# Sixty-four rows of w_down in one load of eight partitions, at the end of a one-token transformer block

## The chip, the cores and the metric

The kernel runs on one core of a Trainium2 chip. The metric is the device time of one execution in microseconds; before the change its median is 407.73 us over 3 runs (407.71 to 407.74). Engines: PE (matrix products, with PEld for its weight loads), DVE (vector), ACT (activation), POOL (general), SP (issues the loads). Loads run on 16 transfer engines that all queues share.

## The reference

One token goes through attention over a cached context of 65,536 positions and then through a gated feed-forward part. All tensors are bf16.

```python
def _A_ref(x, k_cache, v_cache, wq, wo):        # x 1x1x1024, 32 query heads, 4 key heads, Dh = 128
    q = (x @ wq).reshape(B, Sq, Hq, Dh).transpose(0, 2, 1, 3)
    k = jnp.repeat(k_cache, rep, axis=1)
    v = jnp.repeat(v_cache, rep, axis=1)
    scores = jnp.einsum("bhqd,bhkd->bhqk", q, k) * (Dh ** -0.5)
    p = _softmax(scores, axis=-1)
    o = jnp.einsum("bhqk,bhkd->bhqd", p, v)
    return o.transpose(0, 2, 1, 3).reshape(B, Sq, Hq * Dh) @ wo

def _B_ref(x, w_gate, w_up, w_down):            # 1024 -> 3584 -> 1024
    return (_gelu(x @ w_gate) * (x @ w_up)) @ w_down

h = x + _A_ref(_layernorm(x), A_k_cache, A_v_cache, A_wq, A_wo)
h2 = h + _B_ref(_layernorm(h), B_w_gate, B_w_up, B_w_down)
```

## The kernel before, in words

All weights and both caches are read once, 173 MB. SP issues every load (`load`, L172) into `ring`, a buffer of three slots of 64 KB per partition. The order of the loads is fixed by the program: wq, the K and V pieces of 8 MB, wo (8 MB), w_gate and w_up (7 MB each), and then w_down in five pieces. A load waits until the products that read its slot's earlier content are done; the loads behind it on SP wait with it. All w_down pieces lie in the slot that wo had.

PE and DVE work through what has landed: K pieces are transposed by DVE (L288) and multiplied (`k_scores`), V pieces are multiplied with the softmax weights (`v_values`). Each engine works through its instructions in program order, apart from where the tile scheduler puts small independent ones.

The part that matters here is w_down, the last matrix. Its 3584 rows are split so that partition p has rows 28p to 28p + 27; the 28 rows of a partition are called c = 0 to 27. The activations `act_bf` (128 x 28, L544) are copied into `actz` (L547 with `padded`, L235), where each column is followed by 31 zero columns, so that a product gives 32 output rows of which the first counts. A product for one c contracts over the 128 partitions. Four row groups of PE (32 columns of weights each) work side by side: `row_mm` (L468) puts c into group c mod 4.

The order at the end is this:
- `keep_busy(4)`, L578. `keep_busy` (L557) makes products into `w_ps` that nobody reads.
- c = 0 to 15 come in one load (4096 KB, L580). Each c takes two products of 512 columns, which are added into the two banks `at_ps` (L582). These banks already hold the residual and the attention output. The last four c close the sums.
- `keep_busy(3)`, L583.
- `rows_out` (L486) copies the two banks to `sum_r`: DVE copies one, ACT the other (L248).
- Sixteen products with `ones_f` add the four row groups of `sum_r` up and start the sums in `f_ps` and `fb_ps`, one bank for each half of the output (L587).
- `keep_busy(4)`, L588.
- c = 16 to 23 (2048 KB), then `keep_busy(3)`, then c = 24 to 26 (768 KB): `down_rows` (L570) makes eight products of 128 columns for each c, into `f_ps` and `fb_ps`.
- c = 27 comes in two loads, one for each half of the columns (128 KB each, L597). After the first half four products into `f_ps` and a cast by DVE; after the second four into `fb_ps` and a cast by ACT (L601). Then SP stores the row (L602).

All five w_down loads are issued together once wo's slot is free.

Of the kernel before, what the change touches and what calls it, by code (L numbers as in the profile page):

```python
# [9 lines left out]
ALU = mybir.AluOpType  # L10
AX = mybir.AxisListType
BF16 = mybir.dt.bfloat16
F32 = mybir.dt.float32
PSUM = bass.MemoryType.PSUM
# [3 lines left out]
def kernel(  # L18
# [13 lines left out]
    nc = tc.nc  # L32
    P = 128
    D = A_x.shape[-1]
# [4 lines left out]
    F = B_w_gate.shape[1]  # L39
    DC = D // P  # L40
    FC = F // P
# [5 lines left out]
    CW = 16384  # L47
    NSLOT = 3
# [25 lines left out]
    sel = lead.tile([P, 32], F32, name="sel")  # L74
# [9 lines left out]
    o_fin = lead.tile([P, D // 4], BF16, name="o_fin")  # L84
    assert 2048 + 2 * 512 + 2 * 256 + 128 + 2 * 64 + 4 * 32 == ring_at - const_at - 128
    chpool = ctx.enter_context(tc.tile_pool(name="chpool", bufs=1))
    ring = chpool.tile([P, NSLOT * 2 * CW], BF16, name="ring")
    top = ctx.enter_context(tc.tile_pool(name="top", bufs=1))
    wsel = top.tile([P, W0 + NS * P], BF16, name="wsel", tag="wo")
    small = ctx.enter_context(tc.tile_pool(name="small", bufs=2))  # L90
# [1 line left out]
    def pt_tile(i, shape, dtype, name):  # L92
        return (lead if i == 0 else top).tile(shape, dtype, name=name, tag=f"pT{i}")
# [50 lines left out]
    def pe(op):  # L144
        return keep(op, "pe")
# [7 lines left out]
    def mm(out, lhsT, rhs, start, stop, loaded=False, tile_position=None, skip_group_check=False):  # L153
        t = nc.tensor
        if not loaded:
            return pe(t.matmul(out, lhsT=lhsT, rhs=rhs, start=start, stop=stop, tile_position=tile_position,  # L156
                               skip_group_check=skip_group_check))
        op = t.add_instruction(mybir.InstMatmult(  # L158
            name=nc.get_next_instruction_name(), engine=t.engine, start_tensor_calc=start, stop_tensor_calc=stop,
            tile_size=(lhsT.shape[0], lhsT.shape[1]), tile_position=tile_position or (0, 0), ldweights=False,  # L160
            bass_skip_group_check=skip_group_check,
            ins=[t.lower_ap(rhs), t.lower_ap(lhsT, for_matmul_weights=True)], outs=[t.lower_ap(out, opt=True)]))
        reuses.add(op.ins.name)
        return pe(op)
# [4 lines left out]
    slot = [NSLOT - 1]  # L169
    loads, pools, last = [], [], {}  # L170

    def load(src, off=0):  # L172
        n, w = src.shape[1], src.shape[2]
        if off == 0:
            slot[0] = (slot[0] + 1) % NSLOT
        assert off + n * w <= 2 * CW
        o = slot[0] * 2 * CW + off
        tv = ring[:, o:o + n * w].rearrange("p (n w) -> p n w", w=w)
        loads.append(nc.sync.dma_start(out=tv, in_=src).ins)
        return tv  # L180

# [2 lines left out]
    nc.scalar.dma_start(out=x_row[0:97:32, :], in_=A_x[0, 0].rearrange("(g n) -> g n", g=4))  # L184
    assert DC * HD == 2 * CW
    wq_t = load(wq_v[:])

    make_identity(nc, ident_bf[:])
# [12 lines left out]
    for bp in range(4):  # L201
        s0 = 64 * (bp // 2) + bp % 2
        nc.vector.tensor_copy(out=esel[:, bp, :, :],
                              in_=ident_bf[:, s0:s0 + 63:2].unsqueeze(1).to_broadcast([P, 4, 32]))

    one = ctx.enter_context(tc.tile_pool(name="one", bufs=1))
# [28 lines left out]
    def padded(i, vec, ncols, name):  # L235
        t = pt_tile(i, [P, ncols, 32], BF16, name)
        pools.append(nc.gpsimd.memset(t[:], 0.0))
        nc.vector.tensor_copy(out=t[:, :, 0], in_=vec)
        return t
# [7 lines left out]
    def evac(dst, src, k):  # L247
        return nc.vector.tensor_copy(out=dst, in_=src) if k % 2 == 0 else nc.scalar.copy(out=dst, in_=src)  # L248
# [27 lines left out]
    def kv_load(what, g, li, n):  # L276
        t = load((k_v if what == "k" else v_v)[g][:, li * LN:(li + n) * LN, :])
        for u in range(n):
            state[(what, g, li + u)] = t[:, u * LN:(u + 1) * LN, :]
# [130 lines left out]
    for n, u in enumerate(units):  # L410
# [24 lines left out]
        if g == 0 and li == NL - 1:  # L435
            softmax_turn(0)
            softmax_bias(0)
            for i, m in zip((NL - 1, 0, 1, 2), (2, 3, 4, 4)):
# [11 lines left out]
                            pattern=[[-1, OQ], [1, P]], channel_multiplier=-OQ)  # L450
# [8 lines left out]
    actx.close()  # L459
    ps_a = ctx.enter_context(tc.tile_pool(name="ps_a", bufs=2, space=PSUM))  # L460
    ps_w = ctx.enter_context(tc.tile_pool(name="ps_w", bufs=2, space=PSUM))
    ps_f = ctx.enter_context(tc.tile_pool(name="ps_f", bufs=1, space=PSUM))
    DS = D // 512

    def row_bank(name):
        return ps_w.tile([P, 512], F32, name=name, tag="w")

    def row_mm(banks, stat, w2, c, first, last):  # L468
        g = c % 4
        for s in range(DS):  # L470
            mm(banks[s][32 * g:32 * g + 32, :], stat, w2[:, s * 512:(s + 1) * 512], first, last,
               loaded=(s > 0), tile_position=(0, 32 * g), skip_group_check=True)
# [3 lines left out]
    assert Hq * D == 2 * CW  # L476
    at_ps = [ps_a.tile([P, 512], F32, name="at_ps", tag="a") for _ in range(DS)]
    wv = load(wo_v[:])
    for c in range(Hq):
        row_mm(at_ps, o2z[:, c, :], wv[:, c, :], c, c < 4, False)  # L480
# [5 lines left out]
    def rows_out(name):  # L486
        t = low.tile([P, DS, 512], F32, name=name, tag="sc0")
        for s in range(DS):
            last["act"] = evac(t[:, s, :], at_ps[s][:], s)
        return t  # L490
# [18 lines left out]
    def turned(banks, name, tag):  # L509
# [2 lines left out]
            nc.vector.transpose(out=t[:, k, :], in_=banks[k][:, 0:HF * 32])  # L512
        return t[:].rearrange("p k (j i) -> p (k j) i", i=32)[:, :, 0]

    g_banks = [row_bank("wg_ps") for _ in range(2)]
    gv = B_w_gate.rearrange("(p c) n -> p c n", c=DC)
    uv = B_w_up.rearrange("(p c) n -> p c n", c=DC)
# [25 lines left out]
    act_bf = top.tile([P, FC], BF16, name="act_bf")  # L543
    nc.vector.tensor_tensor(out=act_bf[:], in0=turned(u_banks, "wu_t", "sc2"), in1=gl[:], op=ALU.mult)  # L544

    wd_v = B_w_down.rearrange("(p c) n -> p c n", p=P)
    actz = padded(3, act_bf[:], FC, "actz")  # L547
    w_ps = row_bank("w_ps")

    def seen_by_sync(ins):  # L550
        seen = nc.sync.nop()
        for i in ins:
            tc.add_manual_dep(seen.ins, i.name,
                              mybir.DependencyInfo(mybir.DependencyClass.Sync, mybir.DependencyReason.DATA),
                              reason="seen")

    def keep_busy(n, src):  # L557
        for i in range(n):
            mm(w_ps[:], ident_bf[:], src, True, True, loaded=(i > 0))

    HW = D // 2
# [8 lines left out]
    def down_rows(wv, c0, n, bs):  # L570
        for cc in range(n):
            c = c0 + cc
            for g in range(4):
                for b in bs:
                    o = (b if len(bs) > 1 else 0) * HW + g * QW
                    half_mm(b, g, actz[:, c, :], wv[:, cc, o:o + QW], False, c + 1 == FC, loaded=(b > bs[0]))

    keep_busy(4, wu[:, 0, 0:512])  # L578
    c0 = 16
    wv = load(wd_v[:, 0:c0, :])  # L580
    for c in range(c0):
        row_mm(at_ps, actz[:, c, :], wv[:, c, :], c, False, c + 4 >= c0)  # L582
    keep_busy(3, wv[:, 0, 0:512])  # L583
    sum_r = rows_out("sum_r")
    for g in range(4):
        for b in range(2):
# [2 lines left out]
    for sz, nb in ((8, 3), (3, 0)):  # L589
        wv = load(wd_v[:, c0:c0 + sz, :], c0 * D)  # L590
# [3 lines left out]
    assert c0 == FC - 1  # L594
    o_b = o_fin[:].rearrange("p (b j) -> p b j", b=2)
    for b, put in ((0, nc.vector.tensor_copy), (1, nc.scalar.copy)):
        wv = load(wd_v[:, c0:FC, b * HW:(b + 1) * HW], c0 * D + b * HW)  # L597
        down_rows(wv, c0, 1, [b])
        if b == 1:
            seen_by_sync(loads[-8:] + [last["act"].ins] + [x.ins for x in pools])  # L600
        put(out=o_b[0:97, b, :], in_=halves[b][0:97, :])  # L601
    nc.sync.dma_start(out=out[0, 0].rearrange("(b g n) -> g b n", b=2, g=4),  # L602
                      in_=o_b[0:97:32, :, :])
# [30 lines left out]
```

## Time and profile before

| | |
|---|---|
| median of 3 runs | 407.73 us (407.71 to 407.74) |
| profiled execution, its own time | 407.8 us |
| its span, first to last instruction | 406.0 us |
| mean granted PE clock | 0.891 |
| read from memory | 173.02 MB, 426 GB/s over the span |
| PE, DVE, ACT, POOL busy | 73%, 50%, 10%, 2% of the span |
| 4096 KB of w_down first used | 395.56 us |
| last load landed, as the chain of waits has it | 402.84 us |
| store issued | 403.46 us |

Times within the profile count from the start of the span, 0 to 406.0 us. The row of busy tenths cuts the span into 40 slices of about 10 us, and a 9 means 90% or more. "PEclk" is the clock that the throttle granted, in tenths of full speed (in the windows as a fraction). "DMA" is the mean busy share of the 16 transfer engines. In a timeline row, the bracket at the end says how long the engine was idle before and what ended that. "L156" is the helper that makes products, "L158" the same for products that reuse the weights already loaded; so rows are told apart by their tiles: `at_ps`, `w_ps`, `f_ps`, `fb_ps`.

### The profile page before, as it was taken

The numbers are of one execution on the slowest core, as the hardware profiler recorded it, in microseconds if no ns is written. First come the engines' busy times: TensorE is split into PE (matmuls) and PEld (weight loads), VectorE is DVE, ScalarE is ACT, GpSimd is POOL, SyncE is SP. The second block draws the span as 40 slices with busy tenths as digits, with TensorE's granted clock in tenths as the row PEclk, the third lists the DMA queues.
The fourth block names the chain that finished last, engine by engine and source line by source line (L and its number), as shares of the span: only waits on it lengthen the run. The fifth ranks groups of instructions, "written<-read, shape, count | busy, mean of one in ns | idle before, by whom it ended". The sixth has DMA issues, their size and how long they took to land.

```text
span 406.0 us, 2610 instructions
## 1 busy us (share of the span) xinstructions
PE 295.5 (73%) x1519; PEld 59.4 (15%) x681; DVE 203.8 (50%) x186; ACT 40.0 (10%) x62; POOL 7.5 (2%) x17
## 2 busy tenths in 40 slices
PE   0160777758899695979969957997696999646196
PEld 0110111111111110221111113111110211211012
DVE  0210989999839744971595387609943000220210
ACT  1000000023000031100000302000021100100000
POOL 2000000000000000000000000000010000000000
PEclk9995689987899999769999967899999699886689
DMA  9999999999999999999999999999999999999995
GB/s 413 413 413 471 458 413 415 413 466 452 413 421 420 471 439 413 428 420 471 433 420 428 420 465 433 420 435 420 458 433 420 441 420 458 399 442 447 400 423 225
DMA packets 3631, 173.18 MB, mean 427 GB/s; under 512 B 416, under 2 KB 676, under 8 KB 804
## 3 DMA queue, kind: packets, MB, share of 16 engines
q1 hardware_dynamic: 3612, 173.02, 98.7%
q8 instruction: 8, 0.13, 0.1%
q14 instruction: 3, 0.02, 0.0%
q10 hardware_dynamic: 8, 0.00, 0.0%
HBM read 173.02 MB, written 0.00 MB: 426 GB/s over the span
## 4 chain that ended last, share of the span: by engine, by line
DMA 41%; PE 35%; DVE 21%; ACT 2%; issue 1%; ACTq 0%; DVEq 0%
DMA ring<-in_A_k_cache_dram 30%; DVE ring L288 16%; PE acc_ps L158 16%; DMA ring<-in_B_w_down_dram 11%; PE qk_ps L156 6%; PE qk_ps L158 5%; PE acc_ps L156 5%; DVE mx L313 2%; ACT sc L309 2%; DVE pT L346 1%; PE o_ps L156 1%; PE at_ps L156 1%; DVE acc_sb L369 1%; PE at_ps L158 1%; PE nb_ps L156 0%
## 5 line engine op out<-in xcount | busy, mean ns | idle before, releaser
L288 DVE STREAM_TRANSPOSE ring<-ring 128x2048 uint32<-128x2048 uint32 x64 | 142.6, 2279 | 36.9 <-DMA ring<-in_A_k_cache_dram 36.9
L156 PE MATMUL qk_ps<-ring,wsel 128*128 128x512 bf16 x256 | 107.4, 420 | 50.2 <-DVE ring L288 31.2
L158 PE MATMUL qk_ps<-ring,wsel 128*128 128x512 bf16 x256 | 106.6, 416 | 0.0
L158 PE MATMUL acc_ps<-ring,pT 128*128 128x512 bf16 x384 | 105.1, 383 | 0.0
L156 PEld LDWEIGHTS <-wsel 128*128 128x128 bf16 x256 | 27.1, 106 | 157.3 <-issue 140.4
L156 PE MATMUL acc_ps<-ring,pT 128*128 128x512 bf16 x128 | 49.1, 384 | 0.0
L313 DVE TENSOR_REDUCE mx<-qk_ps 128x1 f32<-128x1024 f32 x16 | 19.5, 1220 | 24.7 <-ACT sc L309 18.7
L346 DVE STREAM_TRANSPOSE pT<-pT 128x1024 bf16<-128x1024 bf16 x16 | 19.3, 1228 | 23.8 <-ACT pT L340 23.8
L309 ACT COPY sc<-qk_ps 128x1024 f32<-128x1024 f32 x12 | 12.1, 1012 | 149.5 <-PE qk_ps L158 149.5
L156 PEld LDWEIGHTS <-pT 128*128 128x128 bf16 x128 | 12.8, 100 | 90.7 <-issue 90.6
L369 DVE COPY acc_sb<-acc_ps 32x512 f32<-32x512 f32 x8 | 5.3, 667 | 29.4 <-PE acc_ps L158 29.3
L340 ACT ACTIVATE pT<-sc,nbias 128x1024 bf16<-128x1024 f32 x12 | 13.7, 1141 | 44.9 <-DVE nbias L332 41.9
L156 PE MATMUL wu_ps<-ring,hnz 128*32 128x448 bf16 x32 | 5.9, 729 | 9.0 <-DMA ring<-in_B_w_up_dram 9.0
L156 PE MATMUL ln_tot<-ln_s,ones_f 128*128 128x1 f32 x8 | 1.9, 312 | 13.5 <-DVE ln_s L210 11.7
L156 PE MATMUL q_ps<-ring,xnz 128*32 128x512 bf16 x32 | 5.0, 598 | 8.9 <-DMA ring<-in_A_wq_dram 8.9
L156 PE MATMUL wg_ps<-ring,hnz 128*32 128x448 bf16 x32 | 5.9, 718 | 7.2 <-DMA ring<-in_B_w_gate_dram 7.2
L156 PE MATMUL o_ps<-sel,acc_sb 128*128 128x8 f32 x32 | 6.6, 335 | 5.8 <-DVE rl L383 5.4
L371 ACT COPY acc_sb<-acc_ps 32x512 f32<-32x512 f32 x8 | 4.6, 578 | 58.6 <-DVE acc_sb L369 58.5
L512 DVE STREAM_TRANSPOSE wu_t<-wu_ps 128x448 f32<-128x448 f32 x2 | 1.2, 630 | 14.2 <-PE wu_ps L156 14.2
L261 DVE STREAM_TRANSPOSE q_t<-q_ps 128x512 f32<-128x512 f32 x2 | 1.3, 694 | 13.8 <-PE q_ps L158 13.8
L512 DVE STREAM_TRANSPOSE wg_t<-wg_ps 128x448 f32<-128x448 f32 x2 | 1.2, 628 | 13.4 <-PE wg_ps L156 13.4
L340 ACT ACTIVATE pT<-qk_ps,nbias 128x1024 bf16<-128x1024 f32 x4 | 4.5, 1114 | 29.8 <-PE acc_ps L158 16.8
(108 smaller groups left out, 94.2 us busy)
## 6 DMA issues: line engine op xcount, KB each, us to landing
ring<-in_B_w_gate_dram SPq DMA_DIRECT2D x1, 7168.0 KB, 35.5
ring<-in_B_w_up_dram SPq DMA_DIRECT2D x1, 7168.0 KB, 38.6
ring<-in_B_w_down_dram SPq DMA_DIRECT2D x1, 4096.0 KB, 39.6
ring<-in_B_w_down_dram SPq DMA_DIRECT2D x1, 2048.0 KB, 43.6
ring<-in_B_w_down_dram SPq DMA_DIRECT2D x1, 768.0 KB, 45.0
ring<-in_B_w_down_dram SPq DMA_DIRECT2D x2, 128.0 KB, 44.8
ring<-in_A_k_cache_dram SPq DMA_DIRECT2D x8, 38.6
ring<-in_A_v_cache_dram SPq DMA_DIRECT2D x8, 34.4
```

The lines of the kernel that those rows point to most:

```text
L156: return pe(t.matmul(out, lhsT=lhsT, rhs=rhs, start=start, stop=stop, tile_position=tile_position, skip_group_check=skip_group_check))
L158: op = t.add_instruction(mybir.InstMatmult(name=nc.get_next_instruction_name(), engine=t.engine, start_tensor_calc=start, stop_tensor_calc ...
L261: nc.vector.transpose(out=q_t[:, k, :], in_=q_banks[k])
L288: dv(nc.vector.transpose(out=kt[:, c * w:(c + 1) * w], in_=kt[:, c * w:(c + 1) * w]))
L309: ac(nc.scalar.copy(out=sc[:], in_=flat))
L313: dv(nc.vector.tensor_reduce(out=state[("mx", g)][:, li:li + 1], in_=flat, axis=AX.X, op=ALU.max))
L340: ac(nc.scalar.activation(out=flat, in_=state.pop(("sc", g, li)), func=ACT.Exp, bias=st["nbias"][:, 0:1], scale=scale, accum_out=st["lpart ...
L346: dv(nc.vector.transpose(out=flat, in_=flat))
L369: dv(nc.vector.tensor_copy(out=acc_sb[sl, :], in_=acc[sl, c, :]))
L371: ac(nc.scalar.copy(out=acc_sb[sl, :], in_=acc[sl, c, :]))
L512: nc.vector.transpose(out=t[:, k, :], in_=banks[k][:, 0:HF * 32])
```

## The change

Of c = 27, one row in each of 128 partitions, the rows of the odd partitions (64 rows of 1024 columns, 128 KB) come in a load of their own, issued behind the 4096 KB load. It goes to eight partitions (0, 8, ..., 56), eight rows to each, into the slot that w_gate had. The rows of the even partitions still come last, in two loads of half the columns, now of 64 partitions and 64 KB each.

The activations for the moved rows have to be moved to those eight partitions. A mask `part` spreads column 27 of `act_bf` over eight columns (`act_q`), one product with a 0/1 matrix `spread` gathers them in `act_ps`, and DVE copies them, padded with zeros, to `few`. Eight rows then make sixteen products of 512 columns into `at_ps`, behind `keep_busy(3)` and ahead of the copies to `sum_r`; they now close the sums there. Column 27 of `actz` is set to zero for odd partitions through the mask `even`. `spread`, `part` and `even` are made once, early. The three slots of `ring` become three tiles. The number of products after each of the two last loads stays four.

```diff
-    ring = chpool.tile([P, NSLOT * 2 * CW], BF16, name="ring")
+    ring = [chpool.tile([P, 2 * CW], BF16, name=f"ring{i}") for i in range(NSLOT)]
...
+    ps_s = ctx.enter_context(tc.tile_pool(name="ps_s", bufs=1, space=PSUM))
...
+    KQ = 8
+    KR = P // 2 // KQ
+    KW = P // KQ
+    low_rows = B_w_down.rearrange("(q r c) n -> q r c n", q=KQ, c=2 * FC)[:, :, 2 * FC - 1, :]
+    part = one.tile([P, KR], F32, name="part", tag="gmb")
+    even = top.tile([P, 1], F32, name="even")
+    spread = top.tile([P, P], BF16, name="spread", tag="wo")
+    nc.vector.tensor_reduce(out=part[:], in_=sel[:].rearrange("p (x r t) -> p t r x", r=KR, t=2)[:, 1], axis=AX.X, op=ALU.add)
+    nc.vector.tensor_reduce(out=even[:], in_=sel[:, 0::2], axis=AX.X, op=ALU.add)
+    nc.gpsimd.memset(spread[:], 0.0)
+    ones_at = spread[:, 0:8 * KQ:8]
+    nc.gpsimd.memset(ones_at, 1.0)
+    nc.gpsimd.affine_select(out=ones_at, ...)
+    nc.gpsimd.affine_select(out=ones_at, ...)
...
-    actz = padded(3, act_bf[:], FC, "actz")
+    FL = FC - 1
+    actz = pt_tile(3, [P, FC, 32], BF16, "actz")
+    pools.append(nc.gpsimd.memset(actz[:], 0.0))
+    nc.vector.tensor_copy(out=actz[:, 0:FL, 0], in_=act_bf[:, 0:FL])
+    act_q = one.tile([P, KR], BF16, name="act_q", tag="ln_xc")
+    nc.vector.tensor_tensor(out=act_q[:], in0=part[:], in1=act_bf[:, FL:FC].to_broadcast([P, KR]), op=ALU.mult)
+    nc.vector.tensor_tensor(out=actz[:, FL, 0:1], in0=even[:], in1=act_bf[:, FL:FC], op=ALU.mult)
...
     for c in range(c0):
-        row_mm(at_ps, actz[:, c, :], wv[:, c, :], c, False, c + 4 >= c0)
+        row_mm(at_ps, actz[:, c, :], wv[:, c, :], c, False, False)
+    act_ps = ps_s.tile([P, KR], F32, name="act_ps")
+    mm(act_ps[:], spread[:], act_q[:], True, True)
+    few = padded(1, act_ps[:], KR, "few")
+    lv = ring[(slot[0] + 1) % NSLOT][:, 0:KR * D].rearrange("p (r n) -> p r n", n=D)
+    loads.append(nc.sync.dma_start(out=lv[0:8 * KQ:8], in_=low_rows).ins)
     keep_busy(3, wv[:, 0, 0:512])
+    for r in range(KR):
+        row_mm(at_ps, few[:, r, :], lv[:, r, :], r, False, r + 4 >= KR)
     sum_r = rows_out("sum_r")
...
     for b, put in ((0, nc.vector.tensor_copy), (1, nc.scalar.copy)):
-        wv = load(wd_v[:, c0:FC, b * HW:(b + 1) * HW], c0 * D + b * HW)
+        o = c0 * D + b * HW
+        wv = ring[slot[0]][:, o:o + HW].rearrange("p (c n) -> p c n", c=1)
+        loads.append(nc.sync.dma_start(out=wv[0:P:2], in_=wd_v[0:P:2, c0:FC, b * HW:(b + 1) * HW]).ins)
         down_rows(wv, c0, 1, [b])
```

More of the change, by code (lines that the diff above doesn't have):

```diff
@@ L176, in load @@
         assert off + n * w <= 2 * CW
-        o = slot[0] * 2 * CW + off
-        tv = ring[:, o:o + n * w].rearrange("p (n w) -> p n w", w=w)
+        tv = ring[slot[0]][:, off:off + n * w].rearrange("p (n w) -> p n w", w=w)
         loads.append(nc.sync.dma_start(out=tv, in_=src).ins)
@@ L513, in turned @@
         return t[:].rearrange("p k (j i) -> p (k j) i", i=32)[:, :, 0]
+    KQ = 8
+    KR = P // 2 // KQ
+    KW = P // KQ
+    assert KQ * KR * 2 == P and 2 * KR == KW and KR * D <= DC * F
+    low_rows = B_w_down.rearrange("(q r c) n -> q r c n", q=KQ, c=2 * FC)[:, :, 2 * FC - 1, :]
[7 more added lines that the diff above has]
+    nc.gpsimd.memset(ones_at, 1.0)
+    nc.gpsimd.affine_select(out=ones_at, in_=ones_at, compare_op=ALU.is_ge, fill=0.0, base=0,
+                            pattern=[[-KW, KQ]], channel_multiplier=1)
+    nc.gpsimd.affine_select(out=ones_at, in_=ones_at, compare_op=ALU.is_ge, fill=0.0, base=KW - 1,
+                            pattern=[[KW, KQ]], channel_multiplier=-1)
     g_banks = [row_bank("wg_ps") for _ in range(2)]
@@ L596 @@
     for b, put in ((0, nc.vector.tensor_copy), (1, nc.scalar.copy)):
-        wv = load(wd_v[:, c0:FC, b * HW:(b + 1) * HW], c0 * D + b * HW)
+        o = c0 * D + b * HW
+        wv = ring[slot[0]][:, o:o + HW].rearrange("p (c n) -> p c n", c=1)
+        loads.append(nc.sync.dma_start(out=wv[0:P:2], in_=wd_v[0:P:2, c0:FC, b * HW:(b + 1) * HW]).ins)
         down_rows(wv, c0, 1, [b])
         if b == 1:
-            seen_by_sync(loads[-8:] + [last["act"].ins] + [x.ins for x in pools])
+            seen_by_sync(loads[-9:] + [last["act"].ins] + [x.ins for x in pools])
         put(out=o_b[0:97, b, :], in_=halves[b][0:97, :])
```

## The prediction

> **What bounds the kernel now.** First the page: span, throttle row, transfer row, shares of the chain.
>
> ```profile
> span 406.0 us, 2610 instructions
> ...
> PEclk9995689987899999769999967899999699886689
> DMA  9999999999999999999999999999999999999995
> ...
> DMA 41%; PE 35%; DVE 21%; ACT 2%; issue 1%; ACTq 0%; DVEq 0%
> ```
>
> The transfer engines are full in every slice but the last: the stream sets the time, and what PE and DVE do earlier is hidden as long as loads stay queued. The chain that ended last, in order of time, says where that stops:
>
> ```profile
> 358.13 44.71 DMA ring<-in_B_w_down_dram
> 402.84 0.04 issue
> 402.88 0.27 PE fb_ps L156 x4
> 403.15 0.02 issue
> 403.17 0.27 ACT o_fin L601
> ```
>
> The stream ends at 402.84 and only 0.6 us of computing follows. All that the change adds to PE lies ahead of this point, so I read the timeline from 395 us on for PE's own slack. Columns: start, duration, engine, line, and in brackets the idle time before.
>
> ```profile
> 395.56 0.41 PE L156 MATMUL at_ps<-ring,actz 128*32 128x512 bf16 x4 [0.26 <-DMA ring<-in_B_w_down_dram]
> ...
> 397.07 0.41 PE L158 MATMUL at_ps<-ring,actz 128*32 128x512 bf16 x4
> 397.40 0.10 PEld L156 LDWEIGHTS <-ident_bf 128*128 128x128 bf16 x1 [0.64 <-issue]
> 397.41 0.39 PE L156 MATMUL w_ps<-ring,ident_bf 128*128 128x512 bf16 x1
> 397.52 0.69 DVE L248 COPY sum_r<-at_ps 128x512 f32<-128x512 f32 x1 [2.27 <-PE at_ps L158]
> 397.61 0.59 ACT L248 COPY sum_r<-at_ps 128x512 f32<-128x512 f32 x1 [18.71 <-PE at_ps L158]
> 397.64 0.59 PE L158 MATMUL w_ps<-ring,ident_bf 128*128 128x512 bf16 x2
> 398.27 0.18 PEld L156 LDWEIGHTS f_ps<-sum_r,ones_f 128*32 128x32 f32 x8 [0.77 <-DVE sum_r L248]
> ...
> 399.84 0.09 PEld L156 LDWEIGHTS <-actz 128*32 128x32 bf16 x1 [0.87 <-issue]
> 400.41 0.24 PE L156 MATMUL f_ps<-ring,actz 128*32 128x128 bf16 x4 [0.51 <-DMA ring<-in_B_w_down_dram]
> ...
> 402.23 0.24 PE L156 MATMUL f_ps<-ring,actz 128*32 128x128 bf16 x4
> 402.57 0.25 PE L156 MATMUL f_ps<-ring,actz 128*32 128x128 bf16 x4
> 402.88 0.24 PE L156 MATMUL fb_ps<-ring,actz 128*32 128x128 bf16 x4
> ```
>
> The sixteen rows of the 4096 KB load start when it lands (395.56). The two copies to `sum_r` run beside three filler products of `keep_busy`. PE is ready for the eight-row load at about 399.89 (weights 399.84, then 0.05 as from 402.18 to 402.23) and waits for data to 400.41: 0.52 us of slack. It has none at the three-row load (402.23), and 0.25 at the last half (402.57 + 0.06 = 402.63 against 402.88). PE's slack in the whole tail is 0.77 us.
>
> The same tail by windows, whose columns end with granted clock, transfer share and GB/s:
>
> ```profile
> 400.40:401.40 1.00, 0.99 (x64) 0.85 (x31) 0.00 (x0) 0.00 (x0) 0.00 (x0) 1.00 0.68 273
> 401.40:402.20 0.80, 0.80 (x11) 0.12 (x2) 0.00 (x0) 0.00 (x0) 0.00 (x0) 1.00 0.49 173
> ```
>
> The share falls to a half before the last landing: some of the sixteen transfer engines are finished 1 to 2 us before others.
>
> **The change part by part.**
>
> *Bytes.* They stay 173.02 MB. 128 KB move from the two last loads to a load behind the 4096 KB one. At 426/16 = 26.6 GB/s an engine, 8 KB take 0.31 us. If the eight-partition load uses eight engines, each of them has 16 KB more early and 8 KB less late, the other eight only 8 KB less: the end of the stream moves by +0.31 us if the late engines are among the eight, by -0.31 us if not; on all sixteen it does not move. Ends: -0.31 and +0.31. No row names the late engines; I take 0, so the last half lands at 402.84, at worst at 403.15.
>
> The row says nothing on how eight partitions are shared out. [...]
>
> *Issue.* The new load writes the buffer that w_gate had, so SP waits for w_gate's products (the last starts at 376.31) and the four loads behind it wait too. Before, SP issued five loads in 3.58 us at 355.95; now one there and five around 377 to 381. The queue then still holds w_up (used from 385.91) and the 4096 KB load (used from 395.56): at least 12 us of cover. Without it the gap in the stream would count in full.
>
> *Set-up.* On POOL a memset and two selects on few columns, a 128x128 memset and one for `few` (ident memset 0.21, ident select 0.30, hnz memset 0.31; together about 1.2 us) stand in front of layer norm's power. `spread` can start when `osel` is free (about 352.2), `few` when `o2z` is (357.5 to 357.8); the power starts at 362.13, so nothing moves, and behind it PE waits to 369.01 for w_gate anyway. On DVE two reductions (0.17 each, row of `ln_s`) go in where the stream hides them. Behind `actz` come two short DVE products (0.2 each, to about 395.7), needed at 397.4. Cost 0. The separate tiles leave the waits of the K and V loads as they were: 0.
>
> *The tail on PE.* This is the cost.
> 1. After the sixteen rows the next slot was 397.28 and the filler began at 397.41: 0.13 for the change of weights. Now `act_ps` comes first: the same change and one product of 8 columns, 0.14 in all. Ends: 0 (hidden beside the filler), and 0.26 (four products of `o2_ps`). I take 0.14, the nearest row.
> 2. The three fillers (0.65 from 397.41 to the free slot at 398.06) lay beside the copies. Now they come before the new rows, as cover for DVE's copy of `few`: product at 397.42, copy 0.26 later (as for `o_sb`) and 0.18 to 0.30 long, ready by 397.98. So the fillers end at 398.20; with 0.10 for the weights the first new product starts at 398.30. Were the cover gone, the copy would cost up to 0.6.
> 3. Sixteen products of 512 columns: 32 took 395.56 to 397.28, so 0.054 each, 0.86. DVE's copy of `at_ps` started 1.96 after the first of 32, now 1.10 after the first of 16: 399.40; ACT's 399.49.
> 4. Nothing lies beside these copies now. `sum_r` was used 0.75 after DVE's start: 400.15 instead of 398.27, +1.88 (1.02 up to the new products, 0.86 in them).
> 5. From there the order is as before. Eight rows ready at 399.89 + 1.88 = 401.77, data long there: the slack of 0.52 leaves +1.36. Three rows 1.82 later, 403.59; first half 0.34 later, 403.93; second half 0.06 later, 403.99. Its data came by 403.15 at worst. Against 402.88 that is +1.11; the last cast and the store follow as before.
>
> The profiled execution took 407.8 (span 406.0, 1.8 around it), 0.07 above the median 407.73. I add the difference to the median: 407.73 + 1.11 = 408.84.
>
> *Clock.* PE now stands idle from about 399.4 to 400.15. Idle stretches of 0.51 and 0.39 in this tail kept the clock at 1.00; 9.00 us ahead of 385.91 brought it to 0.50, and so did the thin work from 347.3 to 352.6 (0.07 us busy in the first 2 us). 0.75 us is nearest to the first: 0. Other end: half clock from 400.15 doubles at most the 2.8 us of products in the tail, +2.8.
>
> [...]
>
> **The rivals.**
> - *The stream still sets the end* (not slower). The addition on PE would have to stay below the slack of 0.77 instead of 1.88, by one mechanism: the new products and the copies behind them run beside work that PE does anyway. For it speak the fillers (ten products after 395.56, all at full clock) and that ends of products are modelled; against it, that the engine's order is fixed and each copy needs the last product. It gives 407.73 - 0.31 to + 0.31, 407.4 to 408.0.
> - *Half clock in the tail*: +1.1 to +3.9, 408.9 to 411.6.
> - *The load does not do what it says*: its eight partitions go through one or two engines, 128 KB at 26.6 GB/s = 4.9 us, less 0.31, +4.6 at most: 412.3. The small load of x_row in four partitions shows as 8 packets, two for each row, which speaks for one engine for each partition.
>
> **How the numbers follow.** My forecast 0.78, the stream 0.13, half clock 0.05, one or two engines 0.03, the rest 0.01 (a gain that I don't see). The forecast's own range, from the ends of terms 1 and 2 and about 0.15 for modelled times, is 408.5 to 409.2. A measurement of this kernel can tell about 0.2% from no change, 0.82 us, so 408.55 is the border: about a tenth of the forecast's chance (0.08) lies within it. Slower 0.70 + 0.05 + 0.03 = 0.78, the same 0.08 + 0.13 = 0.21, faster 0.01. The range 408.0 to 409.8 holds the forecast, the upper edge of the second case and part of the half clock, and leaves out under 2 in 10.
>
> **What would show it.** In the changed profile: `sum_r` copies near 399.4 instead of 397.52; the eight rows' first product near 401.8 with no wait on DMA ahead of it; the last `fb_ps` products near 404.0, right behind the `f_ps` ones; PE in place of DMA at the end of the chain; the transfer share at zero before 403.2. Wrong would be: a wait on DMA ahead of the last `fb_ps` product (the stream decides after all), a clock of 0.50 after 400, or a wait of PE for `few`.

## The result, and the profile after

| | before | after |
|---|---|---|
| median, 5 runs each on the same chip | 407.74 us (407.71 to 407.85) | 409.70 us (409.32 to 409.77) |
| profiled execution, its own time | 407.8 us | 409.77 us |
| its span | 406.0 us | 408.0 us |
| first product of the 4096 KB load | 395.56 us | 396.55 us |
| first sums product | 398.27 us | 401.03 us |
| last products into `fb_ps` | 402.88 us | 404.77 us |

The ratio is 1.0046, with a 95% interval of 1.0031 to 1.0061: slower by 1.96 us, where 1.11 had been forecast. The side and the stated range (408.0 to 409.8) hold; of the size, 0.85 us was missing, and the forecast's own range, 408.5 to 409.2, does not hold the result. The page of the changed kernel, with the same rows as before (span, throttle, transfers, shares of the chain):

```profile
span 408.0 us, 2649 instructions
...
PEclk9996798898999899889989988999899699686689
DMA  9999999999999999999999999999999999999994
...
PE 41%; DMA 39%; DVE 16%; ACT 2%; issue 1%; another core or an unknown queue 0%; ACTq 0%; DVEq 0%
```

The transfer engines are as full as before, but PE now leads the chain. Its last pieces, in order of time:

```profile
404.89 0.06 PE f_ps L156 x4
404.95 0.08 PE fb_ps L156 x4
405.03 0.02 issue
405.05 0.27 ACT o_fin L634
```

Before, a DMA piece stood in front of the last `fb_ps` products. Now one product follows the other with no wait: PE sets the end. The timeline of the changed kernel shows what moved (start, duration, engine, line; in brackets the idle time before and its releaser):

```profile
394.48 1.18 DVE L512 STREAM_TRANSPOSE wu_t<-wu_ps 128x448 f32<-128x448 f32 x2 [14.21 <-PE wu_ps L156]
...
396.26 0.09 PEld L156 LDWEIGHTS <-actz 128*32 128x32 bf16 x1 [1.45 <-issue]
396.55 0.41 PE L156 MATMUL at_ps<-ring,actz 128*32 128x512 bf16 x4 [0.35 <-DMA ring<-in_B_w_down_dram]
...
398.40 0.18 PE L156 MATMUL act_ps<-act_q,spread 128*128 128x8 bf16 x1
...
398.44 0.38 PE L156 MATMUL w_ps<-ring,ident_bf 128*128 128x512 bf16 x1
398.62 0.19 DVE L237 CAST few<-act_ps 128x8 bf16<-128x8 f32 x1 [2.37 <-PE act_ps L156]
...
399.18 0.41 PE L156 MATMUL at_ps<-ring,few 128*32 128x512 bf16 x4
...
400.29 0.69 DVE L247 COPY sum_r<-at_ps 128x512 f32<-128x512 f32 x1 [1.48 <-PE at_ps L158]
...
401.03 0.45 PE L156 MATMUL f_ps<-sum_r,ones_f 128*32 128x128 f32 x8 [0.80 <-DVE sum_r L247]
...
402.60 0.24 PE L156 MATMUL f_ps<-ring,actz 128*32 128x128 bf16 x4
...
404.37 0.24 PE L156 MATMUL f_ps<-ring,actz 128*32 128x128 bf16 x4
...
404.71 0.23 PE L156 MATMUL f_ps<-ring,actz 128*32 128x128 bf16 x4
404.77 0.23 PE L156 MATMUL fb_ps<-ring,actz 128*32 128x128 bf16 x4
```

Three differences make up the 1.89 us between the last `fb_ps` products (404.77 against 402.88). From the first `at_ps` product to the first sums it was 2.71 us and is 4.48, +1.77: the work that was forecast. The rest of the tail, from the sums to the last products, is shorter by 0.87 (404.77 - 401.03 = 3.74 against 402.88 - 398.27 = 4.61), mostly waits on data that have gone. And the tail begins 0.99 us later, at 396.55, with a wait on DMA ahead of it; that was not forecast. 0.99 + 1.77 - 0.87 = 1.89.

The late beginning is seen in the windows, too. Columns: busy time of PE, PEld, DVE, ACT and POOL with their instructions, granted clock, transfer share, GB/s. The kernel before:

```profile
388.00:392.00 4.00, 4.00 (x40) 0.83 (x20) 0.00 (x0) 0.00 (x0) 0.00 (x0) 0.81 0.99 426
...
395.00:396.00 1.00, 0.74 (x11) 0.32 (x8) 0.23 (x1) 0.00 (x0) 0.00 (x0) 1.00 1.03 442
396.00:397.00 1.00, 1.00 (x24) 0.25 (x8) 0.00 (x0) 0.00 (x0) 0.00 (x0) 1.00 0.99 426
```

and the changed kernel:

```profile
388.00:392.00 4.00, 4.00 (x32) 0.76 (x16) 0.00 (x0) 0.00 (x0) 0.00 (x0) 0.58 0.91 393
...
395.00:396.00 1.00, 0.77 (x3) 0.00 (x0) 0.93 (x4) 0.00 (x0) 0.00 (x0) 1.00 1.05 285
396.00:397.00 1.00, 0.65 (x10) 0.32 (x8) 0.25 (x3) 0.00 (x0) 0.00 (x0) 1.00 0.84 240
...
403.00:404.00 1.00, 0.84 (x52) 0.55 (x19) 0.00 (x0) 0.00 (x0) 0.00 (x0) 1.00 0.22 80
```

From 395 to 397 the transfer engines' busy share is 1.05 and 0.84 (before: 1.03 and 0.99), but they move 285 and 240 GB/s instead of 442 and 426: less is moved in a similar busy time. The trace's records of single packets, each with its size and its duration, say the same: they take longer. Before, a 16 KB packet of the 2048 KB load took 611 ns and a 32 KB packet 1213; after, beside the new load, up to 1389 and 1771. The last half load landed 403.43 us after the first packet of the first load instead of 401.85.

The first row holds a second difference. The clock of PE came back to full at about 391.3 instead of 389.5 (0.50 up to there, 1.00 behind; worked out from the windows' means, 0.58 and 0.81), so the products of w_up ended later and the weights of `actz` were loaded at 396.26 instead of 395.37. In this profiled execution PE would have begun at about 396.3 even with the data there. The stream was then changed by itself in runs on the chip; the clock was only read, in each run's profile.

### The profile page after: what moved, and what is told of

Its sections match the earlier page's. It is cut to its first block, busy times and chain, and to the rows that moved or that the text cites. A ratio compares the mean times of both kernels' runs of the same rounds, so it can differ in the third digit from the quotient of the medians.

```text
span 408.0 us, 2649 instructions
## 1 busy us (share of the span) xinstructions
PE 296.0 (73%) x1533; PEld 58.3 (14%) x690; DVE 204.2 (50%) x191; ACT 40.0 (10%) x62; POOL 8.6 (2%) x22
## 4 chain that ended last, share of the span: by engine, by line
PE 41%; DMA 39%; DVE 16%; ACT 2%; issue 1%; another core or an unknown queue 0%; ACTq 0%; DVEq 0%
DMA ring<-in_A_k_cache_dram 30%; PE acc_ps L158 16%; DVE ring L287 11%; DMA ring<-in_B_w_down_dram 10%; PE qk_ps L156 8%; PE qk_ps L158 8%; PE acc_ps L156 5%; DVE mx L312 2%; DVE pT L345 1%; ACT sc L308 1%; PE o_ps L156 1%; PE at_ps L156 1%; PE at_ps L158 1%; DVE acc_sb L368 1%; ACT acc_sb L370 1%
## 5 line engine op out<-in xcount | busy, mean ns | idle before, releaser
L156 PE MATMUL o_ps<-sel,acc_sb 128*128 128x8 f32 x32 | 5.6, 302 | 7.2 <-DVE rl L382 6.4
```

## The experiments

The theories were these.
- *PE alone*: the added products and the serial copies cost 1.1, as forecast, and the rest is an accident of the run.
- *Source*: the rows of the new load lie scattered in memory, and this slows the stream.
- *Destination*: the new load, which lands in eight pieces (394.75 to 397.67 us in the changed kernel's trace) and so is taken to run on eight engines, writes partitions 0, 8, ..., 56, and this slows the stream. It has two forms, which some expectations name by letters: D, the eight engines crowd on too few ways into the buffer memory; F, an engine writes partitions that another engine writes in the large loads. Both are the author's suppositions: the trace doesn't name the engine of a packet, and no run shows which engine writes which partitions or how many ways lead into the buffer memory. The expectations also call *Source* S, and name two more: E, any load on eight engines holds the others up; W, the late stream comes from the added work on the engines.

The ratio in each case is to the kernel before on the same chip, with its 95% interval.

### own_ports: the same load into partitions 0, 4, ..., 28

```diff
-    ones_at = spread[:, 0:8 * KQ:8]
+    ones_at = spread[:, 0:4 * KQ:4]
...
-    loads.append(nc.sync.dma_start(out=lv[0:8 * KQ:8], in_=low_rows).ins)
+    loads.append(nc.sync.dma_start(out=lv[0:4 * KQ:4], in_=low_rows).ins)
```

> The changed kernel, with the 64 moved rows in partitions 0, 4, ..., 28 instead of 0, 8, ..., 56; nothing else differs. In the changed kernel's profile the 4096 KB load is first used at 396.55 instead of 395.56, and packets of 16 KB that took 611 ns take up to 1389 ns while the eight-partition load runs. Theory D (the destination: partitions eight apart crowd a part of the write paths): the first product on the 4096 KB load is back near 395.6, the 16 KB packets are back at 611 ns, and only the addition on PE is left, 407.74 + 1.1 = 408.85 us. Theory S (the source: rows 114,688 bytes apart are slow to read): unchanged, first product near 396.5, 409.7 us. Theory E (any load on eight engines holds the others up): unchanged, 409.7 us. [...]

Measured: 408.77 us (408.56 to 410.2, 6 runs) against 407.77, ratio 1.0033 (1.0020 to 1.0045). Its timeline:

```profile
395.51 0.41 PE L156 MATMUL at_ps<-ring,actz 128*32 128x512 bf16 x4 [0.73 <-DMA ring<-in_B_w_down_dram]
...
399.24 0.69 DVE L247 COPY sum_r<-at_ps 128x512 f32<-128x512 f32 x1 [1.47 <-PE at_ps L158]
...
399.99 0.45 PE L156 MATMUL f_ps<-sum_r,ones_f 128*32 128x128 f32 x8 [0.80 <-DVE sum_r L247]
...
403.72 0.23 PE L156 MATMUL fb_ps<-ring,actz 128*32 128x128 bf16 x4
```

and its windows:

```profile
395.00:396.00 1.00, 0.49 (x12) 0.23 (x7) 0.00 (x0) 0.00 (x0) 0.00 (x0) 1.00 1.11 473
396.00:397.00 1.00, 1.00 (x24) 0.25 (x8) 0.00 (x0) 0.00 (x0) 0.00 (x0) 1.00 0.99 426
```

With nothing changed but the partitions, the data are there at 395.51, the rate is 426 GB/s again, and the packets take 611 and 1213 ns as before. The tail on PE is what it was in the changed kernel (4.48 from the first product to the sums). This kernel is what the forecast described, and it costs +1.00 where +1.11 was forecast. E falls, since the load still lands in eight pieces, taken for eight engines.

### near_rows: the new load reads rows 0 to 63, which lie side by side

```diff
-    low_rows = B_w_down.rearrange("(q r c) n -> q r c n", q=KQ, c=2 * FC)[:, :, 2 * FC - 1, :]
+    low_rows = B_w_down[0:P // 2, :].rearrange("(q r) n -> q r n", q=KQ)
```

> The changed kernel, but the eight-partition load reads rows 0 to 63 of w_down, which lie side by side, in place of the 64 rows that it should read 114,688 bytes apart; the destination stays partitions 0, 8, ..., 56. The result therefore uses wrong weights for 64 rows. Theory S (source): first product on the 4096 KB load back near 395.6, 408.85 us. Theory D (destination) and theory E (eight engines): unchanged, near 396.5, 409.7 us.

Measured: 409.57 us (409.51 to 410.4), ratio 1.0051 (1.0036 to 1.0066). The timeline's first product again waits for data:

```profile
395.92 0.09 PEld L156 LDWEIGHTS <-actz 128*32 128x32 bf16 x1 [1.45 <-issue]
396.41 0.41 PE L156 MATMUL at_ps<-ring,actz 128*32 128x512 bf16 x4 [0.55 <-DMA ring<-in_B_w_down_dram]
```

Where the rows are read makes no difference that these runs can tell (409.57 against 409.70). *Source* falls. So does the size of the new load's packets as a cause, which this edit changes as well: 8 of 16 KB in place of 64 of 2 KB.

### load_only: the loads of the change without its work on PE

```diff
-        row_mm(at_ps, actz[:, c, :], wv[:, c, :], c, False, False)
-    act_ps = ps_s.tile([P, KR], F32, name="act_ps")
-    mm(act_ps[:], spread[:], act_q[:], True, True)
-    few = padded(1, act_ps[:], KR, "few")
+        row_mm(at_ps, actz[:, c, :], wv[:, c, :], c, False, c + 4 >= c0)
...
-    for r in range(KR):
-        row_mm(at_ps, few[:, r, :], lv[:, r, :], r, False, r + 4 >= KR)
```

> The changed kernel without what PE got: no gathering product, no copy to few, no sixteen products; the output lacks the 64 moved rows. All loads are as in the changed kernel. If the loads by themselves slow the stream, whatever the reason (D, S or E): first product on the 4096 KB load near 396.5, the last load lands about 1.6 us later than before, 407.74 + 1.6 = 409.3 us. If the later stream belongs to the work on the engines (theory W): 407.7 us, within 0.3.

Measured: 409.07 us (408.99 to 409.26), ratio 1.0034 (1.0021 to 1.0048). Its timeline:

```profile
394.86 0.09 PEld L156 LDWEIGHTS <-actz 128*32 128x32 bf16 x1 [1.45 <-issue]
396.08 0.41 PE L156 MATMUL at_ps<-ring,actz 128*32 128x512 bf16 x4 [1.29 <-DMA ring<-in_B_w_down_dram]
...
398.79 0.45 PE L156 MATMUL f_ps<-sum_r,ones_f 128*32 128x128 f32 x8
...
401.90 0.24 PE L156 MATMUL f_ps<-ring,actz 128*32 128x128 bf16 x4 [1.47 <-DMA ring<-in_B_w_down_dram]
```

The sums follow 2.71 us after the first product, as before. The weights were there at 394.86, so the clock has no part in it: PE waits 1.29 and then 1.47 us for data. The stream alone costs +1.30, and W falls: there is no added work on PE here.

### pe_only: the work on PE without the loads

The added products run on the first eight rows of the 4096 KB load with weights of zero, and the two half loads are whole again.

```diff
-    nc.vector.tensor_reduce(out=part[:], in_=sel[:].rearrange("p (x r t) -> p t r x", r=KR, t=2)[:, 1], axis=AX.X, op=ALU.add)
-    nc.vector.tensor_reduce(out=even[:], in_=sel[:, 0::2], axis=AX.X, op=ALU.add)
+    nc.vector.memset(part[:], 0.0)
+    nc.vector.memset(even[:], 1.0)
...
-    lv = ring[(slot[0] + 1) % NSLOT][:, 0:KR * D].rearrange("p (r n) -> p r n", n=D)
-    loads.append(nc.sync.dma_start(out=lv[0:8 * KQ:8], in_=low_rows).ins)
+    lv = wv
...
-        loads.append(nc.sync.dma_start(out=wv[0:P:2], in_=wd_v[0:P:2, c0:FC, b * HW:(b + 1) * HW]).ins)
+        loads.append(nc.sync.dma_start(out=wv, in_=wd_v[:, c0:FC, b * HW:(b + 1) * HW]).ins)
```

> The changed kernel with the loads of before: column 27 in two half loads of 128 partitions, no eight-partition load. The gathering product, the copy to few and the sixteen products stay in their places, on zeros and on rows that are in the buffer already, so they add nothing. The prediction's sum for PE alone: sums of sum_r at 400.15 instead of 398.27, first product on the eight rows near 401.8, last fb_ps products near 404.0, 407.74 + 1.11 = 408.85 us (408.5 to 409.2). If PE had more slack than I read from its waits (the stream still decides): 407.7. If the later stream belongs to the work on the engines (theory W): 409.7.

Measured: 409.53 us (409.18 to 409.6), ratio 1.0043 (1.0026 to 1.0060), about 0.7 above what was expected. Its timeline shows why:

```profile
396.14 0.37 PEld L156 LDWEIGHTS <-actz 128*32 128x32 bf16 x8 [1.45 <-issue]
396.17 0.41 PE L156 MATMUL at_ps<-ring,actz 128*32 128x512 bf16 x4
...
400.65 0.45 PE L156 MATMUL f_ps<-sum_r,ones_f 128*32 128x128 f32 x8 [0.80 <-DVE sum_r L247]
```

The length of the tail is again 4.48, but it starts at 396.17, and no wait on data stands in front: the weights were late. The clock came back at about 390.7 here and at 388.6 in own_ports. The windows of pe_only and then of own_ports in which it did (the granted clock is the third figure from the end):

```profile
390.00:391.00 1.00, 1.00 (x12) 0.19 (x4) 0.00 (x0) 0.00 (x0) 0.00 (x0) 0.66 1.14 492
...
388.00:389.00 1.00, 1.00 (x12) 0.22 (x4) 0.00 (x0) 0.00 (x0) 0.00 (x0) 0.72 1.21 524
```

So the products of w_up, which begin at 386.32 here and at 385.84 there, ended later; most of that is the clock (2.1 us longer at half speed, about 1.05 us), the rest (about 0.24) the later beginning. 396.17 - 395.51 = 0.66 accounts for the difference of the spans (407.5 against 406.9). So a late clock can do what the slow stream does, once PE has no slack left.

This matters for *PE alone*: without any new load pe_only is only 0.17 us faster than the changed kernel, so the medians don't tell the two causes apart. The spans of the single executions say more. pe_only has 406.6 once and 407.5 three times; own_ports has 406.8 or 406.9 four times, 407.4 and 408.2. The changed kernel has 407.6 to 408.0 in all five: none of them is short. That fits a stream that is late every time, beside a clock that is late some of the time, but the clock was not read in those executions.

### two_paths: the load into partitions 0 to 7

```diff
-    ones_at = spread[:, 0:8 * KQ:8]
+    ones_at = spread[:, 0:KQ]
...
-    loads.append(nc.sync.dma_start(out=lv[0:8 * KQ:8], in_=low_rows).ins)
+    loads.append(nc.sync.dma_start(out=lv[0:KQ], in_=low_rows).ins)
```

> The changed kernel with the 64 rows in the neighbouring partitions 0 to 7; nothing else differs. Dose test of theory D (destination). [...] If only the distance of eight mattered, or the eight engines: 408.8 (no slow packets) or 409.7 us (as the changed kernel). [...]

Measured: 410.4 us (409.91 to 410.68) against 407.75, ratio 1.0063 (1.0049 to 1.0077). The median looks like a stronger dose, but the trace says otherwise: the first product is at 396.44 and the last half landed 403.49 us after the first packet (changed kernel: 396.55 and 403.43). The span is 407.8, within the changed kernel's; the rest of this profiled run's 410.66 lies outside the span, 2.9 us instead of 1.8. If eight neighbouring partitions crowd more than 0, 8, ..., 56, which is the author's estimate and shown by no run, the stream should end well after the changed kernel's; it ends 0.06 us after it.

### own_load_only: the loads of own_ports without the work on PE

```diff
-    loads.append(nc.sync.dma_start(out=lv[0:8 * KQ:8], in_=low_rows).ins)
+    loads.append(nc.sync.dma_start(out=lv[0:4 * KQ:4], in_=low_rows).ins)
...
-    for r in range(KR):
-        row_mm(at_ps, few[:, r, :], lv[:, r, :], r, False, r + 4 >= KR)
```

(and without the gather product and `few`, as in load_only)

> The loads of own_ports (partitions 0, 4, ..., 28), without the gathering product, the copy to few and the sixteen products; the output lacks the 64 moved rows. The stream alone decides: in own_ports the last half landed 0.25 us later than in the kernel before, counted from the first packet. So 407.77 + 0.25 = 408.0 us (407.5 to 408.2). If eight engines slow the others after all: 409.1 us, as load_only.

Measured: 407.97 us (407.79 to 408.53, 10 runs), ratio 1.0007 (0.9998 to 1.0016). The loads in these partitions cost 0.2 us, which the interval does not tell from nothing; in load_only they cost 1.30.

### own_hidden: own_ports with the added work beside other work

The gather product goes behind the eighth row, the sixteen products directly behind the sixteenth, and the fillers after them, beside the copies; of the four fillers behind the sums one is left.

```diff
     for c in range(c0):
         row_mm(at_ps, actz[:, c, :], wv[:, c, :], c, False, False)
-    act_ps = ps_s.tile([P, KR], F32, name="act_ps")
-    mm(act_ps[:], spread[:], act_q[:], True, True)
-    few = padded(1, act_ps[:], KR, "few")
+        if c == 7:
+            act_ps = ps_s.tile([P, KR], F32, name="act_ps")
+            mm(act_ps[:], spread[:], act_q[:], True, True)
+            few = padded(1, act_ps[:], KR, "few")
...
-    keep_busy(3, wv[:, 0, 0:512])
     for r in range(KR):
         row_mm(at_ps, few[:, r, :], lv[:, r, :], r, False, r + 4 >= KR)
+    keep_busy(3, wv[:, 0, 0:512])
...
-    keep_busy(4, wv[:, 0, 0:512])
+    keep_busy(1, wv[:, 0, 0:512])
```

> own_ports with PE's order changed: the gathering product stands behind row 8 of the 16, the sixteen products stand directly behind the 16 rows, ahead of the three fillers, which lie beside the copies to sum_r again, and one filler instead of four stands ahead of the eight rows. Sum: sums of sum_r at 398.27 + 0.2 + 0.9 = 399.4, eight rows ready at 400.5, which is when their data lands: the addition on PE is hidden and the stream decides, 408.0 us (407.6 to 408.3). If the fillers' places don't matter: 408.8 us, as own_ports.

Measured: 408.01 us (407.7 to 408.77, 11 runs), ratio 1.0010 (1.0001 to 1.0019). Its timeline:

```profile
398.79 0.69 DVE L247 COPY sum_r<-at_ps 128x512 f32<-128x512 f32 x1 [1.67 <-PE at_ps L158]
...
398.89 0.59 PE L158 MATMUL w_ps<-ring,ident_bf 128*128 128x512 bf16 x2
...
399.53 0.45 PE L156 MATMUL f_ps<-sum_r,ones_f 128*32 128x128 f32 x8
...
400.70 0.24 PE L156 MATMUL f_ps<-ring,actz 128*32 128x128 bf16 x4 [0.18 <-DMA ring<-in_B_w_down_dram]
```

The fillers stand beside the copies again, `few` is ready before it is needed, and PE waits for the eight rows once more. Of own_ports' 1.00 us, 0.26 is left. It is the fastest complete version with the new load, and it does not beat the kernel before. In its profile the 4096 KB load is used at 395.72 without a wait on data: here, too, the weights came last (395.69).

### four_engines: four partitions with sixteen rows each

Partitions 0, 4, 8 and 12, thirty-two products; the gather product stands as in own_hidden, and the fillers behind the sums and the eight rows are left out.

```diff
-    KQ = 8
+    KQ = 4
...
-    ones_at = spread[:, 0:8 * KQ:8]
+    ones_at = spread[:, 0:4 * KQ:4]
...
-    keep_busy(4, wv[:, 0, 0:512])
-    for sz, nb in ((8, 3), (3, 0)):
+    for sz, nb in ((8, 0), (3, 0)):
```

> own_hidden with the 64 rows in four partitions (0, 4, 8, 12) of sixteen rows each, thirty-two products in place of sixteen, and no fillers behind the sums. In the kernel before, seven of the sixteen transfer engines end 1.4 us or more ahead of the last. If the four engines that this load would use are among these, they have room for the 24 KB more that each gets (1.0 us) and all others carry 8 KB less: the last load lands 0.3 us earlier, 407.4 us. If one of them is a late one, the last load lands up to 1.0 us later: 408.8 us.

Measured: 408.53 us (408.45 to 409.15, 11 runs), ratio 1.0022 (1.0013 to 1.0031). The idea was that the engines that end early would carry the rows. Its timeline shows that this did not come out: PE waits for data at the 4096 KB load, at the eight rows and again at the three rows:

```profile
395.40 0.41 PE L156 MATMUL at_ps<-ring,actz 128*32 128x512 bf16 x4 [0.47 <-DMA ring<-in_B_w_down_dram]
...
401.46 0.24 PE L156 MATMUL f_ps<-ring,actz 128*32 128x128 bf16 x4 [0.70 <-DMA ring<-in_B_w_down_dram]
...
403.28 0.24 PE L156 MATMUL f_ps<-ring,actz 128*32 128x128 bf16 x4 [0.74 <-DMA ring<-in_B_w_down_dram]
```

The new load's four pieces landed at 0, 0.10, 0.44 and 1.59 us, counted from the first of them: so one of the four engines seems to be a late one, and it now has 24 KB more than before (32 KB in this load, 8 KB less behind it). The packets kept their 611 ns, though, and the 4096 KB load came at 395.40: no neighbouring load is slowed in this layout either.

### shifted_paths and upper_paths: every fourth partition again, begun at 4 or at 64

```diff
-    ones_at = spread[:, 0:8 * KQ:8]
+    ones_at = spread[:, 4:4 + 4 * KQ:4]
...
-    loads.append(nc.sync.dma_start(out=lv[0:8 * KQ:8], in_=low_rows).ins)
+    loads.append(nc.sync.dma_start(out=lv[4:4 + 4 * KQ:4], in_=low_rows).ins)
```

> The changed kernel with the 64 rows in partitions 4, 8, ..., 32 in place of 0, 8, ..., 56: eight groups of four partitions again, as in own_ports, each moved on by one. [...] Theory D (crowding: several engines writing to the same few partitions' group): here each group is written by one engine of the small load, so packets stay at 611 ns as in own_ports, first product near 395.5, 408.8 us. Theory F (an engine that writes elsewhere than to the partitions it serves in the large loads, crowded or not): packets up to 1.4 us, first product near 396.5, 409.6 us.

upper_paths has the slice 64:64 + 4 * KQ:4 (partitions 64, 68, ..., 92) in both places.

> The changed kernel with the 64 rows in partitions 64, 68, ..., 92. [...] Theory F: as the changed kernel, packets up to 1.4 us, 409.6 us. [...]

Measured: shifted_paths 409.55 us (409.3 to 409.81) against 407.69, ratio 1.0043 (1.0028 to 1.0058); upper_paths 410.05 us (409.42 to 410.56), ratio 1.0052 (1.0035 to 1.0069). The first product of shifted_paths:

```profile
395.54 0.09 PEld L156 LDWEIGHTS <-actz 128*32 128x32 bf16 x1 [1.45 <-issue]
396.21 0.41 PE L156 MATMUL at_ps<-ring,actz 128*32 128x512 bf16 x4 [0.73 <-DMA ring<-in_B_w_down_dram]
```

and of upper_paths:

```profile
396.92 0.41 PE L156 MATMUL at_ps<-ring,actz 128*32 128x512 bf16 x4 [1.75 <-DMA ring<-in_B_w_down_dram]
```

Both spread the eight rows' partitions as widely as own_ports, and both are slow: the 16 KB packets take up to 1158 and 1124 ns. (In the upper_paths run the stream was already 0.5 us late from earlier loads; the rest, 0.9, is like the others.) D, which asked for packets of 611 ns in shifted_paths, falls. F, which asked for slow ones in both, is the one of these theories that is left, as a supposition: no run shows which engine writes which partitions. All layouts together, from the profiled executions:

| partitions of the new load | kernel | 16 KB packets, at most | `actz` weights loaded | first product | waits for data |
|---|---|---|---|---|---|
| none | before | 611 ns | 395.37 | 395.56 | yes |
| none | pe_only | 611 ns | 396.14 | 396.17 | no |
| 0, 4, ..., 28 | own_ports | 611 ns | 394.84 | 395.51 | yes |
| 0, 4, ..., 28 | own_load_only | 611 ns | 395.14 | 395.47 | yes |
| 0, 4, ..., 28 | own_hidden | 611 ns | 395.69 | 395.72 | no |
| 0, 4, 8, 12 | four_engines | 611 ns | 395.00 | 395.40 | yes |
| 0, 8, ..., 56 | after | 1389 ns | 396.26 | 396.55 | yes |
| 0, 8, ..., 56 | near_rows | 1213 ns | 395.92 | 396.41 | yes |
| 0, 8, ..., 56 | load_only | 1286 ns | 394.86 | 396.08 | yes |
| 0 to 7 | two_paths | 1420 ns | 395.93 | 396.44 | yes |
| 4, 8, ..., 32 | shifted_paths | 1158 ns | 395.54 | 396.21 | yes |
| 64, 68, ..., 92 | upper_paths | 1124 ns | 395.23 | 396.92 | yes |

## Why the prediction was right and wrong

**Bytes: the step that failed.** It let the end of the stream move by +0.31 us at most and took 0. The sum behind it priced the moved bytes at the stream's own rate, as if eight packets more on an engine cost their bytes and nothing else. The last half landed 1.58 us later (403.43 against 401.85), five times the bound, because the other loads' packets beside it took up to 2.3 times as long (1389 against 611 ns). The runs show what decides it: the layout of the destination. Into partitions 0, 4, ..., 28 the same bytes, from the same rows, in the same eight pieces, cost 0.2 us or nothing.

What it is in the layout was not shown. The spacing of the partitions does not decide: own_ports and shifted_paths both take every fourth one (packets of 611 ns and of up to 1158), and two_paths with neighbouring partitions is hardly slower (1420) than the changed kernel (1389). Why a packet slows down stays open. Shown is only that it depends on the layout: two layouts leave the stream alone, four slow it.

**Issue and set-up: right.** No slice shows the transfer share below 0.9 ahead of the tail, though SP waits for a free buffer. From DVE's transposes of w_up to the load of the weights it was 1.80 us (393.57 to 395.37) and is 1.78 (394.48 to 396.26): the two added DVE products cost nothing.

**The tail on PE: right, with small terms off.** Counted from the first `at_ps` product:

| | forecast | measured |
|---|---|---|
| first of the sixteen new products | 2.74 | 2.63 |
| from there to DVE's copy | 1.10 | 1.11 |
| from there to the first sums | 0.75 | 0.74 |
| sum, less the 2.71 of before | 1.88 | 1.77 |
| sums to the eight rows, without a wait | 1.62 | 1.57 |
| eight rows to three rows | 1.82 | 1.77 |
| three rows to the last half | 0.40 | 0.40 |

Term 1 was 0.04 instead of 0.14: the filler began 0.04 after the gather product (398.40 to 398.44). With the data on time the sum's +1.11 becomes 0.9 by these numbers; own_ports measured +0.84 in its profile (403.72 against 402.88) and +1.00 in its median.

**The sum.** With a layout that leaves the stream alone the forecast of +1.11 comes within 0.11 us (own_ports' median, +1.00). The forecast's own tail, begun 0.99 us later and corrected by the 0.21 of the table, gives 403.99 + 0.99 - 0.21 = 404.77, which is the measured place. So one term was left out, the 0.99 at the start of the tail. That 409.70 still lies in the stated range is luck in part: its upper end, 409.8, was put there for half clock in the tail, which did not occur. In this execution the late clock of w_up would have given some 0.75 of it by itself. That the stream is cause enough is shown by load_only, near_rows and shifted_paths, whose weights were loaded 0.5 to 1.2 us before the data came. How often the clock rather than the stream sets the start in executions without a profile stays open.

**Clock: right where it was looked for.** From 394 us on it is 1.00 in every window, the 0.74 us between the copies' start and the sums included. The clock ahead of 392 us was not looked at, and there the kernel had room before (PE's 0.77 us of slack) and has none now.

**The rivals.** That the stream still sets the end did not occur: PE is last and waits for no load behind 396.55. But the stream was late as well, so that both moved. Half clock in the tail did not occur (1.00 in every window from 394 us on), nor did one or two engines (the new load landed in eight pieces). Of the signs, the order of the rows and PE at the end came as said, but all three places came 0.8 to 0.9 us later (400.29, 402.60 and 404.77 instead of 399.4, 401.8 and 404.0), and one was wrong: the transfer share was to be zero before 403.2 and is 0.22 from 403 to 404.

## What to carry to other kernels

A small load is not priced by its bytes alone: price what it does to the packets beside it, and where it needs few partitions, try more than one layout, first the one that left the packets at 611 ns (0, 4, ..., 28 for eight): here the layout decided between nothing that could be told and 1.3 us. Work added to an engine behind the last large load cost here what it exceeded that engine's slack by (1.77 us of work against 0.77 of slack, +1.00 in own_ports); put it ahead of fillers that run beside copies, not behind them (+0.26 in own_hidden). When that slack is spent, every earlier lateness (a clock that comes back late, a slower packet) shows in the time.

## What the runs showed of the hardware that had not been expected

- A 128 KB load of eight partitions made neighbouring packets of 16 KB up to 2.3 times as long (1389 against 611 ns; in two_paths 1420) in four layouts of its partitions, and left them alone in two.
- The PE clock came back from 0.50 to full between 388.6 (own_ports) and 391.3 us (the changed kernel) in the profiled executions, while the products of w_up begin at 385.6 to 386.3 in all of them. Why the delay differs was not shown. The kernel before lies within 0.6 us (407.41 to 408.0 in 27 runs); own_ports, bound by PE, spreads over 1.6 (408.56 to 410.2), which the clock may explain, but only the profiled executions show it.
- The sixteen engines don't end together. In the trace of before, seven land their last piece within 0.7 us of the first and nine 1.6 to 2.1 us after it; of the K load that landed about 59 us into the stream none is late by more than 0.5, and the late ones then grow in number, one by one. The page of the changed kernel has a row of what else the engines carried:

```profile
q8 instruction: 8, 0.13, 0.1%
```

By the queue's name these are eight fetches of instructions; each is a packet of 16 KB. That each makes one engine late by about 1.4 us is inferred from the landings: in the kernel before, the first load that lands behind each of its eight fetches has one late engine more (the ninth late engine appears behind an instruction packet of 8 KB at 87 us). A load on four engines can hold a late one (in four_engines the last of four pieces landed 1.59 us behind the first). Six of the twelve profiled runs have a ninth such packet, at 404 to 410 us. In the changed kernel it came at 408.4, just behind the span, and 1.7 us lay outside the span; in two_paths it came at 409.6, and 2.9 us did. So such a packet alone does not explain the 2.9; its cause stays open.
- In two runs the stream fell behind long before the change's place, by 0.3 to 0.5 us: in pe_only from 40 to 60 us on, where 64 KB packets took up to 2.59 us instead of 2.42, and in upper_paths around 175 to 215 us, with up to 2.55. The cause stays open.
